# Chunk 1's loads behind a second hold, the sums of w_out in one place, v ahead of k, and attention one unit later, in a retention layer with a GELU feed-forward

## Chip, cores and metric

The kernel runs on one core of one Trainium2 chip. The metric is the device time of one execution in microseconds; times below are either such times or moments and lengths within one profiled execution, whose span (first to last instruction) is given.

## What is computed

Retention (a recurrent attention with a decay per head) over 4 batches, 8 heads, 768 steps and a head size of 64, and behind it a feed-forward layer with the tanh form of GELU over 3072 tokens, 512 wide, 2048 inside:

```python
for t in range(S):
    state = gamma[None, :, None, None] * state + np.einsum('bhd,bhe->bhde', k[:, :, t], v[:, :, t])
    y[:, :, t] = scale * np.einsum('bhd,bhde->bhe', q[:, :, t], state)
x = y.transpose(0, 2, 1, 3).reshape(B * S, H * D)
h = x @ w_in
g = 0.5 * h * (1.0 + np.tanh(c * (h + 0.044715 * h * h * h)))
out = g @ w_out
```

All inputs and the output are float32.

## The kernel before

**Tiling.** The 768 steps are cut into six chunks (`c`) of 128. Within a chunk the recurrence is done as products of matrices. For each batch `b`, q and k are converted to float16 and transposed (`att_T`); `mm_A` forms the 128x128 products of k and q, and `ev_A` (L260) multiplies them by the decay mask on VectorE into `a_sb`; `mm_yc` (L271) gives the part of y from the state `st`, `mm_yi` (L284) the part from `a_sb` and v, and `ev_Y` copies y into `xT`, the transposed input of the feed-forward part. `mm_s` and `ev_S` (L308, L325) bring the state forward. `att_AY` and `att_S` bundle these steps for several batches.

**The feed-forward part of a chunk** has two stages for its 512 tokens. M1: for each of 16 blocks `fc` of the inner width, four matmuls into a PSUM tile `h_ps` (two buffers) and a GELU on ScalarE into `g` (L393, L409). M2: the product with `w_out`. Chunk 0 does it directly, as four units for each batch (`units2`, L427). From chunk 1 on `units_w` does it with seven products of half the size in place of eight (L531), in 14 units of 8 matmuls: unit `2n + a` is product `n` for half `a` of the tokens. The seven products need sums of blocks of `g` (`g_sums`, tiles `s_g`, on GpSimd, on VectorE in the last chunk) and sums of blocks of `w_out` (`w_sums(i)` for each quarter `i`, tiles `t_w`, on VectorE, once for the whole kernel), both at L462. Products 0 and 1 start in two PSUM banks, X and Z; product 3 starts Z anew, which needs the sum of product 1 (`o_sb` from `o_ps` and `s_p`, VectorE, L462) to have been taken out.

**Order.** Every engine works through its instructions in the order in which the program gives them. `run(units, after)` writes the order out by hand: behind unit number `i` of a stage it puts the steps listed in `after[i]`. So attention of chunk c+1 is spread among the units of chunk c: in the stage of chunks 2 to 5 units 0 to 15 are M1 and 16 to 29 are M2.

**Loads.** Loads are queued on SyncE (`load(c)`: a block load of q in 16 pieces of 64 KB, from chunk 3 on also a block load of k in 16 pieces, and 256 KB loads of k and v for each batch), and a few on ScalarE's queue (`load1(AC, ...)`). A queue issues in order, and an issue that waits holds up what stands behind it on its engine. Each load signals one of eight semaphores; in the built program a load also waits for the load that had its semaphore before. Which load gets which semaphore follows from the planner's expected order of the loads, not from the data. `hold` (L127) is a copy of a single element on GpSimd into the tile that a load is going to write: the load can't start before the element that is copied is there. In chunk 0 one hold keeps the loads of q and k of chunk 1 behind the arrival of `w_out` quarter 2.

**Conversions.** `prep1` (L175, L188) converts a batch's 256 KB tile to float16, with the decay factors multiplied in where they are needed; `prep_blk` (L175, L177) converts a batch's share of a block load (tiles `q` and `kT`), which VectorE then transposes (L233). The engine is the first argument: `VE` VectorE, `AC` ScalarE, `PO` GpSimd.

Of the kernel before, what the change touches and what calls it, by code (L numbers as in the profile page):

```python
# [16 lines left out]
def kernel(  # L17
# [9 lines left out]
    nc = tc.nc  # L27
    B, H, S, Dh = q.shape
    C = 128
    NCk = S // C  # L30
# [48 lines left out]
    BLK = {"q": (2, 3, 4, 5), "k": (3, 4, 5)}  # L79
# [12 lines left out]
    def ld_tile(nm, c, b):  # L92
        if nm == "q":
            t = ld_all(("q32", c)).rearrange("p (b hp) a d -> p b (hp a d)", b=B)
            return t[:, b].rearrange("p (h d) -> p h d", h=H)
        if (nm, c, b) not in raw:
            raw[nm, c, b] = ld.tile([128, H, Dh], F32, tag=f"{nm}32", bufs=8, name=f"{nm}32")
        return raw[nm, c, b]

    def load1(eng, nm, c, b):  # L100
        eng.dma_start(  # L101
            out=ld_tile(nm, c, b),
            in_=srcs[nm][b, :, c * C:(c + 1) * C, :].rearrange("h p d -> p h d"),
        )

    def load_blk(nm, c):
        t = ld_all((nm + ("32" if nm == "q" else "T32"), c))
        src = srcs[nm].rearrange("b (hp j) s (dd d) -> j dd s (b hp) d", j=2, dd=2)
        for j in range(2):
            for dd in range(2):  # L110
                for a in range(4):
                    p0, t0 = (2 * j + dd) * 32, c * C + a * 32
                    nc.sync.dma_start(
                        out=t[p0:p0 + 32, :, a, :], in_=src[j, dd, t0:t0 + 32]
                    )

    def load(c):
        for nm in "qk":
            if c in BLK[nm]:
                load_blk(nm, c)  # L120
        for b in range(B):
            for nm in "vk" if c in BLK["k"] else "kv":
                load1(nc.sync, nm, c, b)

    def hold(nm, c, b, until):

        nc.gpsimd.tensor_copy(out=ld_tile(nm, c, b)[0:1, 0, 0:1], in_=until)  # L127
# [274 lines left out]
    def g_tile(c, fc):  # L402
        if (c, fc // 8) not in g_sb:
            g_sb[c, fc // 8] = gp.tile([128, 8, B * C], F16, tag=f"g{fc // 8}", name="g")
        r = fc % 8 // 2 * 2
        return g_sb[c, fc // 8][:, r:r + 2]
# [4 lines left out]
    def moe1(c, fc):  # L411
        h_ps = bank("h", shape=(128, B * C), name="h_ps")
        moe1_mm(c, fc, h_ps, 0, B * C)
        gelu(g_tile(c, fc)[:, fc % 2], h_ps)
# [98 lines left out]
    def units_w(c):  # L513
        ps, o_sb, snap = {}, {}, {}
        last = c == NCk - 1

        def bank_of(k, a, new):
            if new:
                if last:
                    ps[k, a] = bank(("o", "h")[a], shape=(128, 2, hw), name="o_ps")[:, 0]  # L520
                else:
                    if a == 0:
                        ps[k] = bank("o", shape=(128, 2, hw), name="o_ps")
                    ps[k, a] = ps[k][:, a]
            return ps[k, a]

        def mm(n, a):
            k, lk, rk, new, stop = PROD[n]
            po = bank_of(k, a, new)
            for fp in range(NP):  # L530
                nc.tensor.matmul(  # L531
                    out=po,
                    lhsT=lhs(c, lk, fp, a),
                    rhs=rhs(rk, fp),
                    start=(new and fp == 0 and (last or a == 0)),
                    stop=(stop and fp == NP - 1),
                    skip_group_check=True,
                )

        def o_tile(b):  # L540
            if b not in o_sb:
                o_sb[b] = op.tile([128, 2, d_model], F32, tag=f"o{b}", name="o_sb")
            return o_sb[b]

        def snap_tile(nm):
            if nm not in snap:
                snap[nm] = op.tile([128, 2, hw], F32, tag=nm, name=nm)
            return snap[nm]

        def ev(n, a0, a1):  # L550
            k = PROD[n][0]
            p = ps[k, a0].unsqueeze(1) if last else ps[k]
            if n in SNAP:
                nc.scalar.copy(out=snap_tile(SNAP[n])[:, a0:a1], in_=p)
            elif n in ADD:
                b, x, nm = ADD[n]
                o = o_tile(b)[:, a0:a1, x * hw:(x + 1) * hw]
                tt(nc.vector, o, p, snap[nm][:, a0:a1], ALU.add)
            else:
                nc.scalar.copy(out=o_tile(1)[:, a0:a1, 0:hw], in_=p)  # L560

        def store(b, a0, a1, n0, n1, eng):
            rows = out.rearrange("(a b t) n -> b t a n", a=2, b=2)
            eng.dma_start(  # L564
                out=rows[b, c * C:(c + 1) * C, a0:a1, n0:n1], in_=o_sb[b][:, a0:a1, n0:n1]
            )

        def unit(n, a):
            mm(n, a)
            if not last:  # L570
                if a == 1:
                    ev(n, 0, 2)
                    if n > 4:
                        store(n - 5, 0, 2, 0, d_model, nc.gpsimd)
            elif n < 6:
                ev(n, a, a + 1)
                if n == 4 and a == 1:
                    store(1, 1, 2, hw, d_model, nc.sync)
                if n == 5:
                    store(0, a, a + 1, 0, d_model, (nc.scalar, nc.sync)[a])  # L580
            elif a == 0:
                ev(n, a, a + 1)
                store(1, 0, 1, 0, d_model, nc.scalar)
            else:
                t, p = o_tile(1)[:, 1], ps["X", 1]
                nc.vector.tensor_copy(out=t[:, 0:hw // 2], in_=p[:, 0:hw // 2])
                nc.scalar.copy(out=t[:, hw // 2:hw], in_=p[:, hw // 2:hw])
                store(1, 1, 2, 0, hw, nc.sync)

        return [(lambda n=n, a=a: unit(n, a)) for n in range(7) for a in range(2)]  # L590

    def run(units, after):
        for i, u in enumerate(units):
            u()
            for f, *args in after.get(i, ()):
                f(*args)

    VE, AC, PO, SY = nc.vector, nc.scalar, nc.gpsimd, nc.sync
# [80 lines left out]
    for fc in range(6, NF):  # L679
        moe1(0, fc)  # L680
        if fc in (8, 10):
            load1(AC, "v", 1, (fc - 8) // 2)

    def units2(c, b, n=4, tag="o"):
        u = [(lambda i=i: moe2(c, b, range(i, i + n), tag)) for i in range(0, NF, n)]
# [5 lines left out]
    def preps(c, b):  # L691
# [15 lines left out]
    run(  # L707
        [u[i % 3][i // 3] for i in range(12)] + u[3],
        {
            3: [(w_sums, 0)],  # L710
            6: [(w_sums, 1)],
            8: [(preps, 1, 0)],
            10: [(att_T, 1, 0), (preps, 1, 1)],
            11: [(att_AY, 1, (), "att", 1, (0,), None)],
# [14 lines left out]
            for fp in range(NF // 2)  # L729
        ],  # L730
        {
            1: [(att_AY, 1, (2,), "o", 1, (3,), VE), (w_sums, 2)],
            2: [(w_sums, 3)],
            3: [(att_S, 1, 2), (g_sums, PO, 1, 0, 4, 0, 1)],
            4: [(att_AY, 1, (3,), "o", 1, (), VE)],
            6: [(att_S, 1, 3)],
# [16 lines left out]
            4: [(att_AY, 2, (0, 1), "h", 2, (2, 3), AC)],  # L753
            7: [(att_S, 2, 0, 1)],
            9: [(att_AY, 2, (2, 3), "h", 2, (), AC), (att_S, 2, 2, 3)],
            10: [(prep_blk, AC, "q", 3, 0)] + [(prep_blk, PO, "k", 3, b) for b in range(B)],
            11: [(prep_blk, AC, "q", 3, 1)],
            12: [(prep_blk, AC, "q", 3, 2)],
            13: [(prep_blk, AC, "q", 3, 3)],
# [4 lines left out]
    for c in range(2, NCk):  # L764
        n, m = c + 1, c + 2
        after = {} if n == NCk else {
            6: [(att_T, n, 0)],
            8: [(att_T, n, 1)],
            12: [(att_AY, n, (), "att", n, (0, 1), None)],
            13: [(att_T, n, 2)],  # L770
            15: [(att_T, n, 3)],
            16: [(prep1, AC, "k", n, 0), (prep1, AC, "k", n, 1)],
            17: [(prep1, AC, "k", n, 2), (prep1, AC, "k", n, 3)],
            18: [(att_AY, n, (0, 1), "h", n, (2, 3), VE)],
            21: [(att_S, n, 0, 1)],
            24: [(att_AY, n, (2, 3), "h", n, (), AC), (att_S, n, 2, 3)],
        }

        def more(at, *what, first=False):
            old = after.get(at, [])  # L780
            after[at] = list(what) + old if first else old + list(what)

        for i in range(4):
            more(4 * i + 3, (g_sums, PO if n < NCk else VE, c, 2 * i, 2 * i + 2), first=True)
        if c == 2:
            more(7, (prep1, PO, "v", n, 0), (prep1, PO, "v", n, 1))
            more(15, (prep1, PO, "v", n, 2), (prep1, PO, "v", n, 3))
        if m < NCk:
            more(0, (load, m))
            for b in range(B):  # L790
                more((19, 21, 23, 26)[b], (prep_blk, AC, "q", m, b))
                more((20, 22, 25, 27)[b], (prep_blk, AC, "k", m, b))
                more(24, (prep1, PO, "v", m, b))
        run([(lambda fc=fc: moe1(c, fc)) for fc in range(NF)] + units_w(c), after)


# [28 lines left out]
```

## Time and profile before

| what | value |
|---|---|
| device time, median of 3 | 231.87 us (231.13 to 234.09) |
| span of the profiled execution | 229.5 us |
| TensorE matmuls busy | 204.5 us, 89% |
| VectorE, ScalarE, GpSimd busy | 107.2, 104.8, 113.4 us |
| mean granted TensorE clock | 0.978 |
| moved by DMA | 33.18 MB, 145 GB/s on average |

In the slices of the span each digit is a fortieth of it, 5.74 us: the busy share in tenths, or the granted clock in tenths. In a line of waits the first name waited for the second: total us, times, the longest. In a timeline line stand the start, the length (of the merged group), the engine, the source line, the operation, the tiles and shapes, the count, and in brackets the idle time of the engine before it and what ended that. `SPq` and `ACTq` are the instructions by which SyncE and ScalarE issue a load or a store. A busy matmul is not one at its peak, because matmuls overlap and their ends are modelled.

Stages of the profiled execution, by TensorE's first matmul in each (chain of waits): M2 of chunk 0 starts at 43.73 us, M1 of chunk 1 at 62.66, M1 of chunk 2 at 103.98, of chunk 3 at 136.66, of chunk 4 at 168.35, of chunk 5 at 199.78.

### The profile page before, as it was taken

Reading aid. Unit: us, or ns where it says so; the run is one execution under the profiler, and the core shown is the slowest. Engines: PE = TensorE matmul, PEld = TensorE weight load, DVE = VectorE, ACT = ScalarE, POOL = GpSimd, SP = SyncE. Lnnn points to the kernel's source line nnn. Section 1 sums busy time; section 2 is a strip of 40 time slices with the busy share of each in tenths; the row PEclk is TensorE's granted clock in tenths of the full one; section 3 lists DMA queues with packets and bytes.
Section 4 is the critical chain, followed back from the end, with each engine's and each line's share of the span. In section 5 each row is a group of like instructions: output and inputs, shape, how many; then the busy total and the mean of one; then the engine's idle time right before and its main releaser. Section 6 shows DMA issues by size and latency. Waiting matters only on the chain.

```text
span 229.5 us, 4764 instructions
## 1 busy us (share of the span) xinstructions
PE 204.5 (89%) x1928; PEld 133.3 (58%) x1928; DVE 107.2 (47%) x213; ACT 104.8 (46%) x186; POOL 113.4 (49%) x115
## 2 busy tenths in 40 slices
PE   7878950999996799999997999998999997999993
PEld 3436620445674577884465884476854586844783
DVE  3543231005889537783086390179550663424421
ACT  2654521404343375226663727684446642176321
POOL 0692001400119559733999965999429992110000
PEclk9999995899999799999999999999999999999999
DMA  7999999924679986699886979869440000030004
GB/s 177 288 237 206 207 200 225 248 63 156 122 142 244 187 126 105 109 257 278 129 126 112 259 151 277 127 97 255 112 183 3 0 3 0 36 150 0 0 3 183
DMA packets 124437, 33.18 MB, mean 145 GB/s; under 512 B 117952, under 2 KB 122432, under 8 KB 124416
## 3 DMA queue, kind: packets, MB, share of 16 engines
q1 hardware_dynamic: 108272, 21.09, 46.1%
q0 software_dynamic: 5456, 8.65, 15.8%
q10 hardware_dynamic: 10688, 3.15, 5.8%
q8 instruction: 15, 0.25, 0.5%
q14 instruction: 6, 0.05, 0.1%
HBM read 30.78 MB, written 6.29 MB: 162 GB/s over the span
## 4 chain that ended last, share of the span: by engine, by line
PE 64%; DMA 12%; POOL 11%; DVE 7%; ACT 2%; SPq 1%; issue 1%; ACTq 0%; DVEq 0%; POOLq 0%
PE h_ps L393 26%; PE o_ps L531 24%; POOL s_g L462 7%; DMA w_out<-in_moe_w_out_dram 7%; PE o_ps L427 6%; DMA k<-in_k_dram 5%; DVE t_w L462 3%; DVE a_sb L260 3%; PE y_ps L271 2%; PE a_ps L247 2%; PE y_ps L284 2%; PE qkT_ps L224 1%; SPq L101 1%; POOL w_in L374 1%; POOL k L188 1%; POOL v L188 1%
## 5 line engine op out<-in xcount | busy, mean ns | idle before, releaser
L393 PE MATMUL h_ps<-xT,w_in 128*128 128x512 f16 (+2 forms) x488 | 90.4, 342 | 13.6 <-ACT g L409 8.4
L409 ACT ACTIVATE g<-h_ps 128x512 f16<-128x512 f32 (+1 forms) x98 | 57.3, 588 | 51.5 <-PE h_ps L393 43.0
L393 PEld LDWEIGHTS <-w_in 128*128 128x128 f16 x488 | 46.5, 100 | 52.4 <-issue 12.1
L260 DVE TENSOR_TENSOR a_sb<-a_ps,mask 128x512 f16<-128x512 f32 x48 | 30.1, 683 | 39.6 <-PE a_ps L247 39.6
L462 POOL TENSOR_TENSOR s_g<-g 128x512 f16<-128x512 f16 x32 | 37.3, 1166 | 18.2 <-ACT g L409 18.2
L531 PEld LDWEIGHTS <-s_g 128*128 128x128 f16 x320 | 30.5, 98 | 8.8 <-issue 2.6
L531 PE MATMUL o_ps<-t_w,s_g 128*128 128x256 f16 x240 | 28.6, 273 | 4.3 <-DVE o_sb L462 2.4
L531 PEld LDWEIGHTS <-g 128*128 128x128 f16 x240 | 23.1, 98 | 3.8
L462 POOL TENSOR_TENSOR s_g<-s_g,g 128x512 f16<-128x512 f16 x16 | 18.6, 1163 | 1.3
L531 PE MATMUL o_ps<-w_out,g 128*128 128x256 f16 x160 | 19.1, 273 | 0.0
L462 POOL TENSOR_TENSOR s_g<-g,s_g 128x512 f16<-128x512 f16 x16 | 18.7, 1168 | 0.0
L300 DVE TENSOR_TENSOR xT<-y_ps,dec 128x512 f16<-128x512 f32 x16 | 10.3, 687 | 17.2 <-PE y_ps L284 17.2
L188 POOL TENSOR_TENSOR v<-v,cst 128x512 f16<-128x512 f32 x16 | 16.3, 1048 | 2.5 <-DMA v<-in_v_dram 2.5
L188 POOL TENSOR_TENSOR k<-k,cst 128x512 f16<-128x512 f32 x8 | 8.4, 1048 | 16.1 <-DMA k<-in_k_dram 16.1
L564 POOL DMA_DIRECT2D out_dram<-o_sb x8 | 5.9, 737 | 18.6 <-DVE o_sb L462 15.2
L427 PE MATMUL o_ps<-w_out,g 128*128 128x512 f16 x64 | 14.8, 379 | 0.0
L177 DVE COPY qkT<-qkT_ps 128x1024 f16<-128x1024 f16 (+1 forms) x9 | 5.1, 572 | 19.6 <-PE qkT_ps L224 19.6
L560 ACT COPY o_sb<-o_ps 128x512 f32<-128x512 f32 (+1 forms) x5 | 2.7, 544 | 23.0 <-PE o_ps L531 23.0
L233 DVE STREAM_TRANSPOSE qkT<-q 128x512 f16<-128x512 f16 x16 | 11.1, 692 | 2.7 <-ACT q L175 2.7
L151 PE MATMUL spin_ps<-zero 128*128 128x512 f16 x32 | 9.9, 446 | 1.2 <-DVE zero L143 1.2
L325 DVE SCALAR_TENSOR_TENSOR st<-st,cst,s_ps 128x128 f16<-128x128 f16 (+1 forms) x40 | 10.1, 313 | 1.1 <-PE s_ps L308 1.1
L427 PEld LDWEIGHTS <-g 128*128 128x128 f16 x64 | 5.9, 97 | 6.6
(54 smaller groups left out, 189.6 us busy)
## 6 DMA issues: line engine op xcount, KB each, us to landing
k<-in_k_dram SPq DMA_DIRECT2D x22, 256.0 KB, 4.4
v<-in_v_dram SPq DMA_DIRECT2D x18, 256.0 KB, 4.4
q<-in_q_dram SPq DMA_DIRECT2D x64, 64.0 KB, 2.8
out_dram<-o_sb POOLq DMA_DIRECT2D x8, 512.0 KB, 3.5
kT<-in_k_dram SPq DMA_DIRECT2D x48, 64.0 KB, 2.6
w_in<-in_moe_w_in_dram POOLq DMA_DIRECT2D x4, 512.0 KB, 9.8
w_out<-in_moe_w_out_dram POOLq DMA_DIRECT2D x4, 512.0 KB, 14.8
v<-in_v_dram ACTq DMA_DIRECT2D x6, 256.0 KB, 4.4
```

What stands on the lines that cost most here:

```text
L151: nc.tensor.matmul(out=ps, lhsT=zero[:, 0:128], rhs=zero, start=True, stop=True)
L188: eng.tensor_tensor(out=t, in0=src, in1=cst[:, col:col + H].unsqueeze(2).broadcast_to([128, H, Dh]), op=ALU.mult,)
L233: nc.vector.transpose(out=t[:, i].rearrange("p hp t -> p (hp t)"), in_=blk16.pop((nm, c, b)).rearrange("p ha d -> p (ha d)"),)
L260: nc.vector.tensor_tensor(out=s, in0=ps[j], in1=mask[:, j], op=ALU.mult)
L300: nc.vector.tensor_tensor(out=x, in0=ps, in1=dec, op=ALU.mult)
L325: nc.vector.scalar_tensor_tensor(out=t[:, :, hp], in0=t[:, :, hp], scalar=cst[:, OG + hp:OG + hp + 1], in1=s_ps[:, :, hp], op0=ALU.mult, o ...
L393: nc.tensor.matmul(out=out, lhsT=w_in_sb[wi][:, kc, wr * 128:(wr + 1) * 128], rhs=xT[c][:, kc, t0:t1], start=(kc == 0), stop=(kc == NHP - ...
L409: nc.scalar.activation(out=out, in_=in_, func=AF.Gelu_apprx_tanh, scale=1.0)
L427: nc.tensor.matmul(out=ps[:, n0:n1], lhsT=g_sb[c, fc // 8][:, fc % 8, b * C:(b + 1) * C], rhs=w_out_sb[fc // (NF // NO)][:, fc % (NF // NO ...
L462: eng.tensor_tensor(out=out, in0=in0, in1=in1, op=op)
L531: nc.tensor.matmul(out=po, lhsT=lhs(c, lk, fp, a), rhs=rhs(rk, fp), start=(new and fp == 0 and (last or a == 0)), stop=(stop and fp == NP ...
L564: eng.dma_start(out=rows[b, c * C:(c + 1) * C, a0:a1, n0:n1], in_=o_sb[b][:, a0:a1, n0:n1])
```

## The change

Five edits of the order; no operation of the computation is added or taken away, and one copy of one element comes in.

- **A second hold**: behind M1's fc=11 of chunk 0, chunk 1's loads of q and k are also made to wait for the GELU of fc=10. It is meant to let v's loads, which stand among the GELUs on ScalarE's queue, come first in the planner's order.
- **Sums of w_out**: all four quarters in M2 of chunk 0, where two of them stood in M1 of chunk 1, ahead of work that TensorE needs.
- **Order within load(c)** for chunks 3 to 5: q block, v, k block, k (before: q block, k block, then v and k in turn).
- **Conversions**: for chunk 3 GpSimd converts v, not kT, in M2 of chunk 1, and ScalarE converts kT among the GELUs of chunk 2; for chunks 4 and 5 kT goes from ScalarE to GpSimd, at the end of the stage. q's conversions on ScalarE move closer together.
- **Attention in M2** of chunks 2 to 4 one unit (tile) later: 19, 22 and 25 in place of 18, 21 and 24, so that the sum of product 1 is issued to VectorE ahead of the attention's evictions.

```diff
--- before.py
+++ after.py
@@ -115,12 +115,17 @@
                     )
 
     def load(c):
-        for nm in "qk":
-            if c in BLK[nm]:
-                load_blk(nm, c)
-        for b in range(B):
-            for nm in "vk" if c in BLK["k"] else "kv":
-                load1(nc.sync, nm, c, b)
+        load_blk("q", c)
+        if c in BLK["k"]:
+            for b in range(B):
+                load1(nc.sync, "v", c, b)
+            load_blk("k", c)
+            for b in range(B):
+                load1(nc.sync, "k", c, b)
+        else:
+            for b in range(B):
+                for nm in "kv":
+                    load1(nc.sync, nm, c, b)
 
     def hold(nm, c, b, until):
 
@@ -680,6 +685,8 @@
         moe1(0, fc)
         if fc in (8, 10):
             load1(AC, "v", 1, (fc - 8) // 2)
+        if fc == 11:
+            hold("q", 1, 0, g_tile(0, 10)[0:1, 0, 0:1])
 
     def units2(c, b, n=4, tag="o"):
         u = [(lambda i=i: moe2(c, b, range(i, i + n), tag)) for i in range(0, NF, n)]
@@ -707,8 +714,10 @@
     run(
         [u[i % 3][i // 3] for i in range(12)] + u[3],
         {
-            3: [(w_sums, 0)],
-            6: [(w_sums, 1)],
+            1: [(w_sums, 0)],
+            2: [(w_sums, 1)],
+            5: [(w_sums, 2)],
+            7: [(w_sums, 3)],
             8: [(preps, 1, 0)],
             10: [(att_T, 1, 0), (preps, 1, 1)],
             11: [(att_AY, 1, (), "att", 1, (0,), None)],
@@ -729,8 +738,7 @@
             for fp in range(NF // 2)
         ],
         {
-            1: [(att_AY, 1, (2,), "o", 1, (3,), VE), (w_sums, 2)],
-            2: [(w_sums, 3)],
+            1: [(att_AY, 1, (2,), "o", 1, (3,), VE)],
             3: [(att_S, 1, 2), (g_sums, PO, 1, 0, 4, 0, 1)],
             4: [(att_AY, 1, (3,), "o", 1, (), VE)],
             6: [(att_S, 1, 3)],
@@ -753,7 +761,7 @@
             4: [(att_AY, 2, (0, 1), "h", 2, (2, 3), AC)],
             7: [(att_S, 2, 0, 1)],
             9: [(att_AY, 2, (2, 3), "h", 2, (), AC), (att_S, 2, 2, 3)],
-            10: [(prep_blk, AC, "q", 3, 0)] + [(prep_blk, PO, "k", 3, b) for b in range(B)],
+            10: [(prep_blk, AC, "q", 3, 0)] + [(prep1, PO, "v", 3, b) for b in range(B)],
             11: [(prep_blk, AC, "q", 3, 1)],
             12: [(prep_blk, AC, "q", 3, 2)],
             13: [(prep_blk, AC, "q", 3, 3)],
@@ -764,33 +772,34 @@
     for c in range(2, NCk):
         n, m = c + 1, c + 2
         after = {} if n == NCk else {
-            6: [(att_T, n, 0)],
-            8: [(att_T, n, 1)],
             12: [(att_AY, n, (), "att", n, (0, 1), None)],
-            13: [(att_T, n, 2)],
             15: [(att_T, n, 3)],
             16: [(prep1, AC, "k", n, 0), (prep1, AC, "k", n, 1)],
             17: [(prep1, AC, "k", n, 2), (prep1, AC, "k", n, 3)],
-            18: [(att_AY, n, (0, 1), "h", n, (2, 3), VE)],
-            21: [(att_S, n, 0, 1)],
-            24: [(att_AY, n, (2, 3), "h", n, (), AC), (att_S, n, 2, 3)],
+            19: [(att_AY, n, (0, 1), "h", n, (2, 3), VE)],
+            22: [(att_S, n, 0, 1)],
+            25: [(att_AY, n, (2, 3), "h", n, (), AC), (att_S, n, 2, 3)],
         }
 
-        def more(at, *what, first=False):
-            old = after.get(at, [])
-            after[at] = list(what) + old if first else old + list(what)
-
+        def more(at, *what):
+            after[at] = after.get(at, []) + list(what)
+
+        if n < NCk:
+            for b in range(B - 1):
+                if c == 2:
+                    more((8, 9, 11)[b], (prep_blk, AC, "k", n, b))
+                more(((9, 10, 13) if c == 2 else (6, 8, 13))[b], (att_T, n, b))
+            if c == 2:
+                more(13, (prep_blk, AC, "k", n, 3))
         for i in range(4):
-            more(4 * i + 3, (g_sums, PO if n < NCk else VE, c, 2 * i, 2 * i + 2), first=True)
-        if c == 2:
-            more(7, (prep1, PO, "v", n, 0), (prep1, PO, "v", n, 1))
-            more(15, (prep1, PO, "v", n, 2), (prep1, PO, "v", n, 3))
+            at = 4 * i + 3
+            after[at] = [(g_sums, PO if n < NCk else VE, c, 2 * i, 2 * i + 2)] + after.get(at, [])
         if m < NCk:
             more(0, (load, m))
             for b in range(B):
-                more((19, 21, 23, 26)[b], (prep_blk, AC, "q", m, b))
-                more((20, 22, 25, 27)[b], (prep_blk, AC, "k", m, b))
+                more((20, 21, 23, 24)[b], (prep_blk, AC, "q", m, b))
                 more(24, (prep1, PO, "v", m, b))
+                more(29, (prep_blk, PO, "k", m, b))
         run([(lambda fc=fc: moe1(c, fc)) for fc in range(NF)] + units_w(c), after)
```

## Prediction

> **What bounds the kernel now.** I read, in this order, the slices of the span, the waits of TensorE, the timeline around the two largest of them, and SyncE's timeline. The slices (one of 40 is 5.74 us):
>
> ```profile
> PE   7878950999996799999997999998999997999993
> PEclk9999995899999799999999999999999999999999
> ```
>
> TensorE is busy in nearly every slice after the start, with two holes: the seventh and eighth slice (34 to 46 us), and the thirteenth and fourteenth (69 to 80 us). The granted clock falls in both, to 0.5 and 0.7. The waits of TensorE alone (reason: total us, times, longest):
>
> ```profile
> PE h_ps L393 <- ACT g L409: 8.4, 3, 7.9
> PE h_ps L393 <- DVE xT L177: 3.8, 1, 3.8
> PE o_ps L531 <- DVE o_sb L462: 2.4, 2, 1.4
> PE o_ps L531 <- POOL s_g L462: 1.9, 1, 1.9
> ```
>
> These four, 16.5 us, are almost all the idle time after the start; TensorE sets the end, and only what shortens them (or the slow clock behind them) shortens the kernel. The timeline of the first hole (start, length, engine, line):
>
> ```profile
> 30.07 0.60 ACT L409 ACTIVATE g<-h_ps 128x512 f16<-128x512 f32 x1 [0.27 <-PE h_ps L393]
> 33.07 0.18 POOL L127 CAST q<-w_out 1x1 f32<-1x1 f16 x1 [14.32 <-DMA w_out<-in_moe_w_out_dram]
> 33.69 0.58 SPq L101 DMA_DIRECT2D k<-in_k_dram  x1
> 38.57 0.43 ACTq L101 DMA_DIRECT2D v<-in_v_dram  x1
> 39.05 1.09 ACT L409 ACTIVATE g<-h_ps 128x512 f16<-128x512 f32 x2 [8.38 <-DMA k<-in_k_dram]
> 39.70 4.04 PE L393 MATMUL h_ps<-xT,w_in 128*128 128x512 f16 x12 [7.94 <-ACT g L409]
> ```
>
> After the gelu of fc=10, ScalarE should issue the load of v(1,1). That issue goes only at 38.57, 0.02 us after k(1,0) has landed (33.69 + 4.86, the chain of waits). The two loads have no data in common. In the built program the loads of SyncE and ScalarE share eight completion semaphores, dealt out in the order in which the planner expects the loads, and each load waits for the former load of its semaphore: v(1,1) got the one of k(1,0). k(1,0) is queued behind the hold, the hold behind w_out[2]. So gelu, then TensorE, waits for a weight. The second hole, on VectorE:
>
> ```profile
> 66.43 0.68 DVE L177 CAST xT<-y_ps 128x512 f16<-128x512 f32 x1
> 67.03 0.75 DVE L462 TENSOR_TENSOR t_w<-w_out 128x512 f16<-128x512 f16 x2
> 67.69 1.85 DVE L462 TENSOR_TENSOR t_w<-w_out,t_w 128x512 f16<-128x512 f16 x2
> 69.46 2.66 DVE L462 TENSOR_TENSOR t_w<-w_out 128x512 f16<-128x512 f16 x2
> 72.05 2.65 DVE L462 TENSOR_TENSOR t_w<-w_out,t_w 128x512 f16<-128x512 f16 x2
> 74.62 0.84 DVE L325 SCALAR_TENSOR_TENSOR st<-st,cst,s_ps 128x64 f16<-128x64 f16 x4
> 75.39 0.68 DVE L177 CAST xT<-y_ps 128x512 f16<-128x512 f32 x1
> ```
>
> The last xT of chunk 1, without which the second half of its M1 can't begin, stands behind eight sums of w_out, which grow from 0.4 to 1.4 us each as GpSimd starts its s_g sums at 68.11. The loads' pace, on SyncE:
>
> ```profile
> 56.09 10.22 SPq L113 DMA_DIRECT2D q<-in_q_dram  x16
> 75.04 9.26 SPq L113 DMA_DIRECT2D q<-in_q_dram  x16
> 104.06 11.05 SPq L113 DMA_DIRECT2D q<-in_q_dram  x16
> 132.15 11.40 SPq L113 DMA_DIRECT2D q<-in_q_dram  x16
> ```
>
> Each line opens the loads of a chunk (2 to 5). SyncE issues without a break, 28 to 29 us a chunk: nearly a chunk's time (31.7 us). Loads have slack now, but can become the bound.
>
> **What the skill says.** "TensorE: Matmul & The Clock Gate", section "What's actually happening": an idle window of about 3.4 us halves the array's clock until it has been busy for as long. The trace agrees: behind the 7.94 us gap 12 matmuls of 512 columns take 4.04 us (337 ns each), behind it 44 take 9.50 us (216 ns each). "SBUF — State Buffer", section "Who interferes with whom": a VectorE operation with two SBUF inputs and a GpSimd operation that reads SBUF exclude each other. The trace agrees: 0.42 us a sum alone, 1.37 to 1.39 us beside s_g. "DMA: Bandwidth & Descriptors", section "Issuing engines are not separate DMA queues": loads from several engines share the same DMA engines. In 30 to 40 us the DMA share is full at 213 GB/s, so moving a load there delays others.
>
> **The change, part by part.**
>
> *Second hold.* One more GpSimd copy of one element (0.18 us) between the hold on w_out[2] and the loads of q and k of chunk 1. It waits for the gelu of fc=10, done at 30.67, before w_out[2] lands at 33.0; so in fact it costs 0.2 us. What it changes is the planner's order: in the built program v(1,0) and v(1,1) now stand ahead of q(1,0), and v(1,1) waits for a load of the start, long landed. Gelu of fc=11 follows at 30.9, and the matmuls of fc=13 at 31.76 at full clock, instead of at 39.70 at the low one: 7.94 + (4.04 - 12 x 0.216 = 1.45) = **9.4 us**, all on TensorE's path; M2 of chunk 0 starts near 34.3 instead of 43.7.
> Price: v(1,1), v(1,2), v(1,3) go ahead of or among q and k. 256 KB at 213 GB/s is 1.2 us, so k(1,0) lands about 2.5 us later, near 41, k(1,3) near 48. First transposes on TensorE now stand 9.7, 12.3, 15.6 and 18.3 us behind the start of M2, so at 44.0, 46.6, 49.9, 52.6; with 1.04 us for GpSimd's product, k is ready near 42, 44, 47.5, 49. At nothing, then; bounds 0 and 2 us.
>
> *Sums of w_out in M2 of chunk 0.* The 8 late sums take 0.42 us each while VectorE waits (it stood idle for 5.85 us up to 37.74, and for 15.35 us before 53.78), and GpSimd runs few products there. In M1 of chunk 1 they leave: xT for batch 3 then follows its y_ps (69.3) at once, before the first half's matmuls end near 72.4. TensorE's wait of 3.75 us goes, and with it the slow clock: 24 matmuls of 256 columns took 4.46 us instead of 24 x 0.109 = 2.6 us (the chain shows 16 such in 1.75 us at full clock). Together 3.75 + 1.85 = **5.6 us**.
>
> *v products ahead of k blocks.* For chunk 3, GpSimd converts v in M2 of chunk 1 (4 x 1.04 us, where 4 x 0.61 us of kT leave, and it then idles to 103.27), so that two pairs of v products, of which one stood in the chain (2.00 us at 117.46), leave the s_g sums of chunk 2. That removes the **1.9 us** wait on s_g. The kT casts move into ScalarE's gelus of M1 in chunk 2: 4 x 0.62 us into gaps of 0.27 us behind each gelu. Worst lag behind 8, 9, 11, 13 is about 0.7 us, TensorE's double buffer has 0.2 us of it free: it costs **0.5 us** (bounds 0 and 1.2). From chunk 3 kT casts are GpSimd's, at a chunk's end: behind the store's issue (1.7 us into the next M1) 2.3 us of casts end about where s_g begins, 4.2 us into M1: **0.4 us** if kT comes a little late (bounds 0 and 1).
>
> *Attention one tile later.* TensorE's wait for o_sb comes from four a_sb products (2.39 us on VectorE) ahead of the sum that empties the Z bank. Behind unit 19 that sum is issued before them: **2.4 us** (1.0 and 1.4 in chunks 3 and 4). The four a_sb have six tiles (6 x 0.87 us) until they are used, as before: at nothing.
>
> *Loads earlier.* All this pulls the work of chunk 2 forward by 15 us, the loads only by about 9 (SyncE goes on when M2's first results are stored, 53.01 now). For q(4): last issue 115.1, landing 2.8 us later, less 9: 109; its first cast on ScalarE stands at about 89 + 18 = 107 (chunk 2's start at 104 less 15, and unit 20). It waits 2 us, but the next evacuation queued behind it is due only at 110.5. k(2,0) has 3 us left, kT(3) 6 us, as kT now comes before k. Nothing on the path, by 1 to 3 us.
>
> Sum (in span and time alike): 9.4 + 5.6 + 1.9 + 2.4 = 19.3 us gained, 0.9 us given back: 18.4 us. 231.87 - 18.4 = **213.5 us**.
>
> **Rivals.**
> A: loads become the bound. For it: the loads move 6 us less than the work, and slacks shrink to 1 to 3 us. Against: no load is needed earlier than that by more than I found. Some 4 us over chunks 2 to 4: 217.5 us.
> B: chunk 1's k comes late. For it: a full DMA in 30 to 40 us and three v loads among q and k; then TensorE waits for its transposes and loses clock again. 5 us of wait and 1.5 of clock: 220 us. Against: 2 us of room for each batch.
> C: nothing is given back, casts and all hide: 212.6 us or a little less.
> D: slower. If ScalarE, now with kT in M1, stood before an unlanded load in each chunk, all gains of 18.4 us would be eaten, and clock losses of 1.4 us for each of four gaps come on top: 237.5 us. Against: kT(3) should land at 92, ScalarE asks at 97; in chunks 3 to 5 the casts are GpSimd's.
>
> **How the numbers follow.** Forecast 0.62, A 0.20, B 0.07, C 0.08, D 0.03. The range takes in C with 1.5 us to spare below, A and the upper bounds of the unknown costs (2 + 0.7 + 0.6 us) above: 211 to 219.5. Only D is not faster by 2% (227.2): faster 0.95, within 2% 0.02, slower 0.03.
>
> **What would show it.** Right: no gap of ScalarE behind fc=10, matmuls of fc=13 near 31.8 and no clock below 0.9 from 20 us on; no t_w sum after 40 us; none of the four waits above 0.5 us; chunk 2 starts near 89, chunks 2 to 4 take 30 to 31 us each. Wrong: TensorE waiting for transposes of chunk 1 near 44, for ScalarE behind a kT or q cast, or a new wait on s_g in chunks 3 and 4.

## The result, and the profile after

The changed kernel takes 212.24 us (median of 4 runs, 211.43 to 213.56), the kernel before 232.56 us beside it (231.13 to 234.09). The ratio is 0.913 with a 95% interval of 0.905 to 0.922. The forecast was 213.5 us with a range of 211 to 219.5. The profiled span went from 229.5 to 209.7 us, by 19.8 us. Ratios compare only runs within 1.5% of the quickest of their kernel, which leaves out 13 of the 20 runs of `sums_only` and one of the four of `new_order_old_conv` below; the two kernels that ran once have no ratio.

The slices of the span after the change, to be laid beside those of before:

```profile
PE   7789999999998999999999999999999999999992
PEclk9999999999999999999999999999999999999999
```

Both holes are closed and the clock no longer falls. TensorE's waits after the change, from 20 us to the end of the span, which are these two alone (reason: total us, times, longest us):

```profile
PE qkT_ps L229 <- ACT k L180: 1.3, 3, 0.5
PE h_ps L398 <- ACT g L414: 0.5, 2, 0.2
```

All four waits that the prediction showed are gone or at 0.5 us; that of the transposes for k's conversion grew from 0.8 to 1.3 us. The first hole, in the timeline (start, length, engine, line):

```profile
28.80 0.60 ACT L414 ACTIVATE g<-h_ps 128x512 f16<-128x512 f32 x1 [0.27 <-PE h_ps L398]
28.81 0.38 ACTq L101 DMA_DIRECT2D v<-in_v_dram  x1
29.66 0.60 ACT L414 ACTIVATE g<-h_ps 128x512 f16<-128x512 f32 x1 [0.27 <-PE h_ps L398]
...
33.36 0.44 POOL L132 CAST q<-w_out 1x1 f32<-1x1 f16 x1 [14.44 <-DMA w_out<-in_moe_w_out_dram]
33.86 0.27 POOL L132 CAST q<-g 1x1 f32<-1x1 f16 x1
...
34.57 0.59 SPq L101 DMA_DIRECT2D k<-in_k_dram  x1
```

v(1,1) is issued at 28.81, as soon as the GELU of fc=10 has started, and the next GELU follows after the usual 0.27 us. The trace's records of semaphores agree with the prediction's account: before, the issue of v(1,1) waits for the semaphore that k(1,0) signals; after, it waits for none. The second hold comes when its element has long been there: it takes 0.27 us, and k(1,0) is issued 0.9 us later than before, where the prediction had 0.2; 0.3 us of it is `w_out` quarter 2, which landed later in this run (33.31 and 33.02). The second hole, on VectorE:

```profile
33.33 0.76 DVE L467 TENSOR_TENSOR t_w<-w_out 128x512 f16<-128x512 f16 x2 [1.51 <-DMA w_out<-in_moe_w_out_dram]
...
36.71 0.76 DVE L467 TENSOR_TENSOR t_w<-w_out 128x512 f16<-128x512 f16 x2 [1.83 <-DMA w_out<-in_moe_w_out_dram]
...
58.68 0.69 DVE L182 CAST xT<-y_ps 128x512 f16<-128x512 f32 x1 [0.81 <-PE y_ps L289]
```

The late sums run at 0.4 us each as soon as their quarter of `w_out` has landed, and the last xT follows its y_ps. SyncE's first loads of chunks 2 to 5:

```profile
46.83 10.59 SPq L113 DMA_DIRECT2D q<-in_q_dram  x16
...
64.86 9.84 SPq L113 DMA_DIRECT2D q<-in_q_dram  x16
...
94.94 8.77 SPq L113 DMA_DIRECT2D q<-in_q_dram  x16
...
121.56 12.15 SPq L113 DMA_DIRECT2D q<-in_q_dram  x16
```

The loads moved forward by 9.1 us (chunk 4) and 10.6 us (chunk 5), the start of chunk 3's M1 by 17.6.

The stages of the two profiles and of the experiments below, from TensorE's first matmul of one stage to that of the next, in us (from the timeline; the last column runs to the end of the span):

```
kernel              first M1  M1 c0  M2 c0  M1 c1  M2 c1  chunk 2  chunk 3  chunk 4  rest
before              17.99     25.58  19.03  24.00  17.22  32.67    31.69    31.44    29.88
changed             16.72     16.20  19.02  18.83  17.22  30.92    30.59    29.86    30.34
hold_only           16.95     16.20  19.02  24.71  17.22  32.66    31.69    31.44    29.81
sums_only           18.26     25.65  19.03  18.83  17.22  36.54    31.69    31.44    29.84
hold_sums           18.16     16.20  19.03  18.83  17.22  39.57    31.70    31.43    29.86
v11_late            18.16     16.20  19.02  24.98  17.22  32.65    31.69    31.44    29.84
after_old_att       16.99     16.20  19.02  18.83  17.22  32.03    31.69    31.44    30.28
after_old_loads     16.88     16.19  19.03  18.83  17.22  38.52    30.60    29.86    29.87
old_order_new_conv  17.99     16.20  19.03  18.83  17.22  32.65    37.29    29.86    29.83
new_order_old_conv  17.16     16.20  19.02  18.83  17.22  39.65    30.61    29.86    30.35
after_kT_VE         17.23     16.19  19.03  18.83  17.22  31.38    30.60    29.86    30.26
after_again         18.17     16.20  19.28  18.82  17.22  30.93    30.60    29.88    30.31
sums_behind         18.62     25.90  19.03  22.12  18.37  32.66    31.68    31.44    29.87
pool_late           17.13     27.83  19.20  24.64  17.22  32.65    31.69    31.44    29.87
```

The first column varies by 1.9 us between runs, with the arrival of `w_in`; nothing in it was edited, and 1.27 us of the 19.8 stand there. Where no edit reached them the other stages repeat within 0.3 us, so they tell more than the totals do. The exceptions are the two stages with a hole: M1 of chunk 0 took 25.58 to 27.83 us in the four kernels that have it, M1 of chunk 1 24.00 to 24.98. The first hole ends when k(1,0) lands, however early M1 began: in `pool_late` M1 began at 17.13, k(1,0) landed at 38.74, and TensorE waited 9.0 us, against 17.99, 38.55 and 7.9 in the kernel before. So an early start lengthened the hole there instead of shortening the kernel.

### The profile page after: what moved, and what is told of

Same layout as the page of the kernel before. It is cut to its first block, busy times and chain, and to the rows that moved or that the text cites. A ratio compares the mean times of both kernels' runs of the same rounds, so it can differ in the third digit from the quotient of the medians.

```text
span 209.7 us, 4776 instructions
## 1 busy us (share of the span) xinstructions
PE 200.6 (96%) x1928; PEld 132.0 (63%) x1928; DVE 104.1 (50%) x213; ACT 101.9 (49%) x182; POOL 115.4 (55%) x120
## 4 chain that ended last, share of the span: by engine, by line
PE 81%; SPq 6%; ACT 4%; DMA 4%; DVE 2%; issue 1%; ACTq 1%; DVEq 0%
PE h_ps L398 35%; PE o_ps L536 29%; SPq L113 5%; PE o_ps L432 5%; PE a_ps L252 3%; PE y_ps L289 3%; PE y_ps L276 2%; DMA iden<-rr_ident 2%; DMA v<-in_v_dram 2%; PE qkT_ps L229 2%; PE spin_ps L156 1%; SPq L101 1%; PE s_ps L313 1%; ACT g L414 1%; ACTq L101 1%
## 5 line engine op out<-in xcount | busy, mean ns | idle before, releaser
L398 PE MATMUL h_ps<-xT,w_in 128*128 128x512 f16 (+2 forms) x488 | 87.4, 334 | 0.5 <-ACT g L414 0.5
L398 PEld LDWEIGHTS <-w_in 128*128 128x128 f16 x488 | 45.3, 97 | 37.4 <-issue 2.8
L536 PE MATMUL o_ps<-t_w,s_g 128*128 128x256 f16 x240 | 27.8, 273 | 0.0
L536 PEld LDWEIGHTS <-g 128*128 128x128 f16 x240 | 23.4, 98 | 3.6
L467 POOL TENSOR_TENSOR s_g<-s_g,g 128x512 f16<-128x512 f16 x16 | 18.4, 1153 | 1.3
L536 PE MATMUL o_ps<-w_out,g 128*128 128x256 f16 x160 | 18.6, 273 | 0.0
L467 POOL TENSOR_TENSOR s_g<-g,s_g 128x512 f16<-128x512 f16 x16 | 18.5, 1153 | 0.0
L569 POOL DMA_DIRECT2D out_dram<-o_sb x8 | 5.9, 737 | 20.3 <-DVE o_sb L467 16.8
L238 DVE STREAM_TRANSPOSE qkT<-kT 128x512 f16<-128x512 f16 x12 | 8.1, 678 | 15.0 <-ACT kT L180 9.5
L559 ACT COPY s_u<-o_ps 128x512 f32<-128x512 f32 (+1 forms) x6 | 3.1, 514 | 17.6 <-issue 9.9
L156 PE MATMUL spin_ps<-zero 128*128 128x512 f16 x32 | 9.4, 429 | 1.2 <-DVE zero L148 1.2
```

The costliest lines, as they stand in the source:

```text
L156: nc.tensor.matmul(out=ps, lhsT=zero[:, 0:128], rhs=zero, start=True, stop=True)
L238: nc.vector.transpose(out=t[:, i].rearrange("p hp t -> p (hp t)"), in_=blk16.pop((nm, c, b)).rearrange("p ha d -> p (ha d)"),)
L398: nc.tensor.matmul(out=out, lhsT=w_in_sb[wi][:, kc, wr * 128:(wr + 1) * 128], rhs=xT[c][:, kc, t0:t1], start=(kc == 0), stop=(kc == NHP - ...
L467: eng.tensor_tensor(out=out, in0=in0, in1=in1, op=op)
L536: nc.tensor.matmul(out=po, lhsT=lhs(c, lk, fp, a), rhs=rhs(rk, fp), start=(new and fp == 0 and (last or a == 0)), stop=(stop and fp == NP ...
```

## Experiments

**The second hold alone.**

```diff
         if fc in (8, 10):
             load1(AC, "v", 1, (fc - 8) // 2)
+        if fc == 11:
+            hold("q", 1, 0, g_tile(0, 10)[0:1, 0, 0:1])
```

> The kernel before with the second hold alone. Theory (the load of v(1,1) stood on ScalarE's queue, ahead of the GELU of fc=11, waiting for the semaphore it shared with k(1,0)): that wait of 8.4 us goes, with it TensorE's 7.9 us and 1.45 us of slow clock: 9.4 us less, about 223 us, and M2 of chunk 0 starts near 34 us instead of 43.7. Rival (chunk 1's q and k come later by the hold, and TensorE waits for them in M2): less than 6 us gained, with a wait of TensorE for transposes of chunk 1.

221.24 us against 233.19 (0.952, 0.945 to 0.960). M1 of chunk 0 is 9.38 us shorter, as in the changed kernel; M1 of chunk 1 is 0.7 us longer, since the slow clock in its hole covers more (24 matmuls took 5.30 us, 4.46 before). The theory holds, and the rival falls: TensorE has no wait for k or q of chunk 1. The medians are further apart, by 11.95 us. The profile of before is of an execution of 231.29 us, near the lowest of that kernel's runs (231.24 to 234.19 beside this one); a hole that is longer in others, as in `pool_late`, would account for the rest, but those were not profiled.

**The same gain without the hold.** The load moves out of the way of the GELUs:

```diff
-        if fc in (8, 10):
+        if fc == 8:
             load1(AC, "v", 1, (fc - 8) // 2)
...
+    load1(AC, "v", 1, 1)
     load1(AC, "v", 1, 2)
```

> The kernel before, no second hold; the load of v(1,1) moves on ScalarE's queue from between the GELUs of fc=10 and fc=11 to behind that of fc=15. It still waits for the semaphore of k(1,0), but no GELU stands behind it. Theory: the same gain as from the second hold, 9.4 us, about 223 us, with ScalarE idle at that load until k(1,0) lands near 38.6 us. Rival (the second hold helps by its delay of the loads, or by relieving the DMA engines): no gain here, about 232 us.

222.70 us (0.957, 0.951 to 0.963), M1 of chunk 0 again 16.20 us. ScalarE's timeline:

```profile
33.69 0.60 ACT L409 ACTIVATE g<-h_ps 128x512 f16<-128x512 f32 x1 [0.27 <-PE h_ps L393]
34.56 0.60 ACT L409 ACTIVATE g<-h_ps 128x512 f16<-128x512 f32 x1 [0.27 <-PE h_ps L393]
38.41 3.57 ACTq L101 DMA_DIRECT2D v<-in_v_dram  x3
42.03 0.62 ACT L175 CAST v<-v 128x512 f16<-128x512 f32 x1 [6.87 <-DMA v<-in_v_dram]
```

The load still stands until 38.41, just behind the landing of k(1,0) at 38.39, but all GELUs have gone by. So the delay that the hold brings is not what helps: it is that nothing TensorE needs stands behind a waiting load. The hold's use is that it changes which load shares a semaphore with which.

**The sums alone**, and **hold and sums together** (the edits of the change; nothing else).

```diff
-            3: [(w_sums, 0)],
-            6: [(w_sums, 1)],
+            1: [(w_sums, 0)],
+            2: [(w_sums, 1)],
+            5: [(w_sums, 2)],
+            7: [(w_sums, 3)],
...
-            1: [(att_AY, 1, (2,), "o", 1, (3,), VE), (w_sums, 2)],
-            2: [(w_sums, 3)],
+            1: [(att_AY, 1, (2,), "o", 1, (3,), VE)],
```

> The kernel before with all four quarters of the sums of w_out in M2 of chunk 0, nothing else. Theory: TensorE's 3.75 us wait for xT in M1 of chunk 1 goes with its 1.85 us of slow clock: 5.6 us less, about 227 us; the eight sums take 0.42 us each in the new place. The first hole (8.4 us) stays. Rival (another work of VectorE or a load ends last in M1 of chunk 1): under 2 us less, with a new wait near 72 us.

> Second hold and sums together. Theory (the two holes are apart, so their gains add up): 15.0 us less, about 217.5 us. Rival (loads become the bound once work moves forward by 15 us and loads by 9 us): less than 12 us gained, with waits for q or k of chunks 2 and 3.

Sums alone: 231.97 us, the median of 20 runs from 227.8 to 234.3, against 233.19 (0.989, 0.984 to 0.993). Together: 223.31 us (0.959, 0.951 to 0.966), no better than the hold alone. Yet M1 of chunk 1 is 5.17 us shorter in both, as in the changed kernel. The gain is lost again in chunk 2: 36.54 and 39.57 us where 32.67 were. So my expectations were wrong. The rival of the pair, that loads come late, is right in kind, though the load in question is kT of chunk 4 and not one of chunks 2 or 3; the rival of the sums alone has the total, but looked for the loss in M1 of chunk 1. In hold and sums together, the timeline of chunk 2:

```profile
109.87 0.62 ACT L175 CAST q<-q 128x512 f16<-128x512 f32 x1 [2.15 <-DMA kT<-in_k_dram]
...
118.37 0.62 ACT L175 CAST kT<-kT 128x512 f16<-128x512 f32 x1 [7.88 <-DMA kT<-in_k_dram]
118.90 0.58 ACT L554 COPY s_u<-o_ps 128x512 f32<-128x512 f32 x1
119.53 1.86 PE L531 MATMUL o_ps<-t_w,s_g 128*128 128x256 f16 x8 [4.00 <-ACT s_u L554]
```

ScalarE comes to the first kT cast of chunk 4 8 us ahead of its load. s_u, which empties the bank that TensorE needs next, stands behind it; TensorE waits 4.00 us and its next matmuls run at the low clock. With the sums alone the same wait is there and shorter:

```profile
PE o_ps L531 <- ACT s_u L554: 2.2, 1, 2.2
```

Why does the hold alone, which moves more work, lose nothing? It moves the loads too. In the profiles chunk 2 starts 9.7 us earlier than before with the hold, 4.8 with the sums and 14.4 with both; the last piece of chunk 4's kT lands 8.5, 0.5 and 8.3 us earlier (126.40 before; 117.95, 125.90 and 118.12). Work runs ahead of this load by 1.3, 4.3 and 6.1 us, and chunk 2 grows by 0.0, 3.9 and 6.9.

**The changed kernel again**, as the measure for the three kernels below that start from it (loads and conversions, attention, kT on VectorE):

> The changed kernel itself, beside the next three on one chip: 212 us.

213.00 us against 231.75 (0.919, 0.916 to 0.922).

**The changed kernel without its loads and conversions**: the order in `load`, the engine and place of the v, kT and q conversions and the places of `att_T` are those of before; hold, sums and later attention stay.

```diff
-        load_blk("q", c)
-        if c in BLK["k"]:
-            for b in range(B):
-                load1(nc.sync, "v", c, b)
-            load_blk("k", c)
...
+        for nm in "qk":
+            if c in BLK[nm]:
+                load_blk(nm, c)
...
-                more((20, 21, 23, 24)[b], (prep_blk, AC, "q", m, b))
+                more((19, 21, 23, 26)[b], (prep_blk, AC, "q", m, b))
+                more((20, 22, 25, 27)[b], (prep_blk, AC, "k", m, b))
                 more(24, (prep1, PO, "v", m, b))
-                more(29, (prep_blk, PO, "k", m, b))
```

> The changed kernel with the old order within the loads and the old conversions (k block ahead of v; kT of chunk 3 on GpSimd, v of chunk 3 between the s_g sums; kT of chunks 4 and 5 on ScalarE). Theory: the 1.9 us wait for s_g in chunk 2 comes back, the slow-down of ScalarE's GELUs by kT (0.5 us) goes: 1.4 us more, 213.6 us. Rival (with the work 15 us earlier the old load order is late): waits for kT, k or v in chunks 2 to 4, over 3 us more, 215.5 us or above.

217.76 us (0.939, 0.933 to 0.946): 4.8 us more than the changed kernel, by medians; its four runs spread from 215.93 to 218.98, and the profile is of one of 218.79. There chunk 2 takes 38.52 us, 7.6 more. TensorE's waits:

```profile
PE o_ps L531 <- ACT s_u L554: 4.0, 1, 4.0
PE o_ps L531 <- POOL s_g L462: 2.0, 1, 2.0
```

Both waits are in chunk 2: that for s_g is the old one, that for s_u the one seen above. The theory named only the first; the rival, that the old order is late, is right. This edit of the change does far more than I priced it at.

**Which half of it?** Starting from the kernel just shown, first only kT of chunks 4 and 5 to GpSimd (`more(29, (prep_blk, PO, "k", m, b))`), then only the new order within `load`. Before measured 233.19 us beside both.

> As after_old_loads (old order within the loads), but kT of chunks 4 and 5 is cast by GpSimd at the end of the stage, as in the changed kernel. Theory (TensorE's 4.0 us wait came from s_u queued on ScalarE behind a kT cast whose load had not landed): that wait is gone. GpSimd's v products wait for v, now last in the loads, until about 124 us, and the kT casts and s_g of chunk 3 start behind them, so 0 to 3 us come back there: 214 to 217 us. Rival (the pace of the loads alone decides): 217.5 us as with the old casts.

> As after_old_loads (old conversions: kT of chunks 4 and 5 cast by ScalarE in M2, kT of chunk 3 by GpSimd ahead of chunk 2), but with the new order within the loads, q, v, kT, k. Theory: kT lands 4 us later than in the old order while ScalarE asks for it as early, so s_u and TensorE wait 4 us longer in chunk 2, 8 us in all, and 1.5 us of clock: 221 to 223 us. Rival (v first is what helps): 214 us or less.

New conversions, old order: 220.65 us (0.948, 0.942 to 0.955). The wait for s_u is gone, as the theory said, but the loss moves to chunk 3, 37.29 us, and is larger than I allowed. GpSimd's timeline:

```profile
126.23 1.04 POOL L188 TENSOR_TENSOR v<-v,cst 128x512 f16<-128x512 f32 x1 [1.63 <-DMA v<-in_v_dram]
127.21 1.47 POOL L564 DMA_DIRECT2D out_dram<-o_sb  x2
128.68 2.27 POOL L177 CAST kT<-kT 128x512 f16<-128x512 f32 x4
...
130.93 1.14 POOL L462 TENSOR_TENSOR s_g<-g 128x512 f16<-128x512 f16 x1
```

The last v, which the old order loads last, holds up two stores, the kT casts and the s_g sums of chunk 3, which start 9.0 us after its M1 (121.92) where the changed kernel has them 4.4 us after (123.31 and 118.91). TensorE waits 4.2 us for them, beside the old 1.8 us in chunk 2.

New order, old conversions: 222.10 us (0.957, 0.948 to 0.967). The total is as the theory had it, the way is not. GpSimd now has to cast kT of chunk 3 ahead of chunk 2's sums, and kT comes later:

```profile
92.65 2.28 POOL L182 CAST kT<-kT 128x512 f16<-128x512 f32 x4 [12.03 <-DMA kT<-in_k_dram]
...
96.36 1.16 POOL L467 TENSOR_TENSOR s_g<-g 128x512 f16<-128x512 f16 x1
```

TensorE's waits in chunk 2, the longest of those for s_g 4.2 us:

```profile
PE o_ps L536 <- POOL s_g L467: 5.1, 2, 4.2
PE o_ps L536 <- ACT s_u L559: 1.2, 1, 1.2
```

So neither half does it alone: v must land before GpSimd asks for it, and whoever casts kT must ask later. A third part, the exchange of v and kT of chunk 3 between GpSimd and ScalarE, has no run of its own; nor have the two halves together without it.

**The changed kernel with attention at its old units.**

```diff
-            19: [(att_AY, n, (0, 1), "h", n, (2, 3), VE)],
-            22: [(att_S, n, 0, 1)],
-            25: [(att_AY, n, (2, 3), "h", n, (), AC), (att_S, n, 2, 3)],
+            18: [(att_AY, n, (0, 1), "h", n, (2, 3), VE)],
+            21: [(att_S, n, 0, 1)],
+            24: [(att_AY, n, (2, 3), "h", n, (), AC), (att_S, n, 2, 3)],
```

> The changed kernel with attention in M2 at its old units (18, 21, 24). Theory: the wait of TensorE for o_sb, behind four a_sb products on VectorE, comes back in each of chunks 2 to 4: 1.0 to 1.4 us each, 2.4 to 4 us more, 215 us. Rival (VectorE has room now): no such wait, 212 us.

215.63 us (0.932, 0.928 to 0.935), 2.6 us more than the changed kernel; chunks 2, 3 and 4 are 1.1, 1.1 and 1.6 us longer, which is 3.8 us, but in its profile M1 of chunk 0 also began 1.2 us earlier than in `after_again` (16.99 and 18.17). TensorE's wait is back:

```profile
PE o_ps L536 <- DVE o_sb L467: 3.5, 3, 1.4
```

**kT of chunk 3 on VectorE.**

```diff
-                    more((8, 9, 11)[b], (prep_blk, AC, "k", n, b))
+                    more((8, 9, 11)[b], (prep_blk, VE, "k", n, b))
...
-                more(13, (prep_blk, AC, "k", n, 3))
+                more(13, (prep_blk, VE, "k", n, 3))
```

> The changed kernel with the four kT casts of chunk 3 on VectorE instead of ScalarE. Theory (those casts push ScalarE's GELUs and TensorE by 0.3 to 0.5 us in M1 of chunk 2): M1 of chunk 2 0.3 to 0.5 us shorter, total 211.8 us. Rival (a VectorE copy shuts GpSimd's s_g sums out): s_g sums longer than 1.15 us, chunk 2 not shorter.

213.04 us (0.919, 0.917 to 0.922): no gain. ScalarE's push on M1 is gone (14.66 us from TensorE's first M1 matmul to its first of M2, 14.94 in the changed kernel), but TensorE waits 0.6 us for s_g, and chunk 2 is 0.5 us longer in all. The casts in chunk 2 (duration min/median/max in ns):

```profile
L182 DVE CAST kT<-kT x4: 1221/1282/1381, 94.3 to 104.1; 128x512 f16<-128x512 f32 x4
...
L467 POOL TENSOR_TENSOR s_g<-g x8: 1140/1242/1343, 93.0 to 109.7; 128x512 f16<-128x512 f16 x8
```

Beside GpSimd's sums the cast takes 1.28 us (0.61 on ScalarE), and the sums rise from 1.15 to as much as 1.34 us. The rival is right. That the sums rise fits what the Trainium skill says in "SBUF — State Buffer", section "Who interferes with whom", of copies and casts on VectorE that use its second port; no run here times this cast with GpSimd idle, or shows which ports it used.

**Place in the queue, or clash with GpSimd?** Two kernels, run once each, ask what made the hole in M1 of chunk 1. In the first the late sums stand behind the last xT and state update; in the second chunk 1's first s_g sums are written one step group later, to let VectorE run alone.

```diff
-            1: [(att_AY, 1, (2,), "o", 1, (3,), VE), (w_sums, 2)],
-            2: [(w_sums, 3)],
+            1: [(att_AY, 1, (2,), "o", 1, (3,), VE)],
...
-            6: [(att_S, 1, 3)],
+            6: [(att_S, 1, 3), (w_sums, 2), (w_sums, 3)],
```

> The kernel before with the sums of quarters 2 and 3 still in M1 of chunk 1, but queued on VectorE behind the last xT and state update of chunk 1, so still beside GpSimd's s_g sums. Theory (the place in VectorE's queue made TensorE wait): the 3.8 us wait for xT is gone although the sums still take up to 1.4 us each. Rival (the clash with GpSimd itself costs TensorE the time): a wait of 3 us or more stays in M1 of chunk 1. The total is near sums_only (231 to 232 us), as the loads' pace in chunk 2 is the same.

```diff
-            3: [(att_S, 1, 2), (g_sums, PO, 1, 0, 4, 0, 1)],
+            3: [(att_S, 1, 2)],
...
-            7: [(g_sums, PO, 1, 4, 8, 0, 1)],
+            7: [(g_sums, PO, 1, 0, 4, 0, 1), (g_sums, PO, 1, 4, 8, 0, 1)],
```

> The kernel before with the first s_g sums of chunk 1 moved back from unit 3 to unit 7 of M1, so that VectorE's eight sums run alone, in their old place ahead of xT. Theory: they take 0.42 us each, 3.4 us in place of 8.9, xT is ready near 72 us and the 3.8 us wait of TensorE is under 0.5 us; place and clash were both needed for the hole. In exchange s_g of chunk 1 comes some 5 us later and TensorE waits for it in M2 of chunk 1, 3 to 6 us; total 230 to 235 us. Rival (place alone): the wait for xT stays above 2 us.

The first took 231.45 us in its one run. VectorE:

```profile
70.29 0.69 DVE L177 CAST xT<-y_ps 128x512 f16<-128x512 f32 x1 [0.81 <-PE y_ps L284]
72.39 0.86 DVE L325 SCALAR_TENSOR_TENSOR st<-st,cst,s_ps 128x64 f16<-128x64 f16 x4 [1.41 <-PE s_ps L308]
73.16 1.11 DVE L462 TENSOR_TENSOR t_w<-w_out 128x512 f16<-128x512 f16 x2
...
79.37 2.66 DVE L462 TENSOR_TENSOR t_w<-w_out,t_w 128x512 f16<-128x512 f16 x2
```

The sums are as slow as before, and TensorE's wait for xT is gone: the place made the wait. The sums then hold up a transpose's eviction (TensorE waits 2.5 us for it, in two waits), and M1 of chunk 1 still takes 22.12 us, so they do need a place where VectorE is idle. The second took 233.45 us and tells nothing of this: GpSimd was idle, so the s_g sums started with their data as before (69.68 us, 5.5 us into M1, as before), the sums took 1.33 us each, the wait for xT was 3.8 us. A later place in the queue delayed nothing here, since the engine was idle and the data came later still. What the hole would be with the sums at 0.42 us in their old place stays open.

## Why the prediction was right

The total was 1.3 us off, and the time lay in the range. The forecast took 18.4 us off; the medians differ by 20.3, the profiles by 19.8, and by 18.5 without the first column. That the sum agrees so well is in part luck: errors of up to 0.5 us in the terms cancel. Step by step, from the table of stages:

- **Second hold**: forecast 9.4 us, measured 9.38 in the profile (M1 of chunk 0), by the hold and, without it, by moving the load out of the way, so the load's wait for a shared semaphore, ahead of the GELUs, is shown as its cause. The three v loads cost nothing, as forecast.
- **Sums**: forecast 5.6 us, measured 5.17. Place in the queue is shown as the cause of the wait; the rest of the difference is about what k's conversion now costs in the second half of this stage (TensorE's waits for it there went from 0.32 to 0.77 us); that this is the cause is argued, not tested.
- **v products ahead of k blocks**: this term was mis-sized. I priced the part as 1.9 us gained less 0.5 and 0.4 us given back, 1.0 us. Beside the kernel before that came out: chunk 2 gained 1.75 us, and ScalarE's push on M1 costs the 0.3 us that its removal showed (of 0.5). But the comparison that counts is with the old loads in a kernel that is 15 us ahead, and there the part is worth 4.8 us in time and 7.6 us in the profile of chunk 2. Without it chunk 2 is longer by 3.9 us with the sums alone (36.54 against 32.67) and by 6.9 us with hold and sums (39.57), which is more than all that the sums gain.
- **Loads earlier**: my rival A, the loads as the bound, I checked only against the new order. For that order the answer was right: no load makes TensorE wait. For the old order it would have been wrong, and the trace of before had the sign of it: ScalarE stood 4.0 us at its first kT cast of chunk 4 in the line below, and s_u followed behind it, with only 0.5 us between them. The line names a_sb, of which the cast has no use. It was the load that ended the wait: its last piece landed at 126.40, 0.25 us before the cast, and the same 0.25 us lie between that landing and this cast in the profiles of `hold_only` (117.95 and 118.20), `sums_only` (125.90 and 126.15) and `hold_sums` (118.12 and 118.37).

```profile
126.65 0.62 ACT L175 CAST kT<-kT 128x512 f16<-128x512 f32 x1 [4.03 <-DVE a_sb L260]
127.79 0.59 ACT L554 COPY s_u<-o_ps 128x512 f32<-128x512 f32 x1 [0.52 <-PE o_ps L531]
```

- **Attention one tile later**: forecast 2.4 us, measured 1.1 + 1.6 us in chunks 3 and 4 and, undone in the changed kernel, 2.6 us in time (3.8 us in chunks 2 to 4 of the profile); chunk 2's share of 1.1 us shows only once its wait for s_g is gone.
- **kT on GpSimd at a chunk's end**: forecast 0.4 us lost in chunk 3, none measured: the s_g sums of chunk 3 start 4.4 us after its M1, after the change (123.31 and 118.91) as before it (140.90 and 136.49).
- **No term for the end**: the last column grew by 0.5 us. The last copy ends as long after M1 of chunk 5 began as before; the 0.5 us lie behind it, and their cause is open.

The total was right because all parts came together. Had hold and sums been proposed without the new order and conversions, the same working would have forecast 5.6 us on top of the hold, where none was to be had (223.31 us against 221.24 with the hold alone).

## What to carry to other kernels

A load queued on a compute engine waits for more than its data: look what its completion semaphore was last used for, and keep such loads off the queue in front of work that sets the pace. When a hole is closed, everything behind it asks earlier for its loads; before adding gains up, subtract the shift from every load's slack, and look for a wait that is harmless now with a bank's evacuation queued behind it. Moving a step later in the program moves it in time only if its engine is busy or its data late.

## What was not expected

- Gains of two edits did not add: 9.4 us and 5.2 us, each seen in its own stage, gave 223.3 us together where the hold alone gave 221.2.
- A late load costs TensorE more than its wait: 4.0 us of wait for s_u lengthened chunk 2 by 6.9 us in the hold-and-sums kernel (39.57 against 32.67), with the matmuls behind it at the low clock (the first 8 took 1.86 us; 16 took 1.92 us just ahead of the wait).
- A float32 cast of 128x512 on VectorE, beside GpSimd's sums, took 1.28 us, twice its 0.61 us on ScalarE.
